# Whole-array attention and gate products in a fused windowed-attention and routed-MoE kernel

## The chip, the cores and the metric

The kernel runs on one core of a Trainium2 chip. The metric is device microseconds of one launch, the median of three runs. Before the change that is 237.91 us (237.64 to 238.76). The engines are named as the profile names them: PE is TensorE (PEld its weight loads), DVE is VectorE, ACT is ScalarE, POOL is GpSimd and SP is SyncE. A product means one matrix multiply instruction of PE; it multiplies a stationary operand, brought in by a weight load of its own, with a moving operand, and the number of partitions that both cover is called its rows here.

## The reference

```python
# q, k, v: (8, 8, 576, 64); window 32; scale 1/8
scores = where(abs(i - j) <= 32, scale * q @ k.T, -1e9)
attn   = softmax(scores)            # with + 1e-9 in the divisor
x      = (attn @ v)  ->  (4608, 512)     # 8 batches of 576 tokens, 8 heads of 64
# routed MoE: D=512, 8 experts, F=1024, 2 modalities
logits = x @ w_gate + modality_bias[modality_id]
e      = argmax(logits);  g = softmax(logits)[e]
out    = g * (relu(x @ w1[e]) @ w2[e])
```

The bias by modality is large beside the logits. The kernel works from the guess that all tokens of a modality go to the expert that the bias favours, flags any token or value that breaks its assumptions, and keeps a slow path behind that flag (attend and forward, from line 920), which the profiled execution does not enter.

## The kernel before

**Attention.** A batch has 8 heads, handled in two groups g of four (one load of q and one of k each), and in pairs of heads. Operation l loads a group as bf16 rows from POOL's queue, and t (L582) transposes it on DVE in 32x32 blocks. SA and SB (scores, L614) are the score products: 32 rows each (a head's 64 values lie as 32 rows times two columns), four heads side by side in the four row strips, with keys on the output partitions. Keys are cut in five blocks of 128 per head. For odd heads the blocks start 64 positions earlier, since 576 is four and a half blocks: the even head's last block holds keys in its first 64 partitions only, and the odd head's first block in its last 64 only. The other 64 partitions of such a block are the dead half. sa and sb (exps) take the exponential on ACT from PSUM into the probability tile pt; sb has a second activation (L625) for each head's block at the end of the tile (slot NM - 1), which is the half-dead one for even and odd heads alike. The scores of the six first pairs are masked by adding a band of large negative numbers in PSUM first (MA, MB, L591 and L595); from pair 6 on, M (L639) multiplies pt with a 0/1 band on DVE.

**V** (L659) multiplies the probabilities with the values: 18 products for a pair of heads, the probabilities stationary and 65 columns moving (64 values and a one, which gives the softmax sum). Two of the 18 cover the half-dead blocks and take 64 rows only, by the slice k_ of line 658. They are not neighbours: in the order of issue a product of 128 rows lies between them and follows each. v (L669, L670) takes the reciprocal and scales on DVE into x.

**Sorting.** The tokens of each 128-token block are sorted by modality: H (L679) multiplies x with a one-hot matrix (o, L573 on POOL or L576 on DVE), and a (L697) copies the result on ACT to a place in the table xl that depends on the counts. J and j (L710, L718) do the same with four rows of token codes, into the code table cl, which has 4 partitions and 4736 columns.

**MoE.** G (L748, L751) is the gate: for each 128 tokens four products of 128 rows and 8 columns, and one of 4 rows and 1 column that decodes the token's code from cl with the weights wi. There are 37 such groups, four to a G but for the last. r and E are the small softmax steps behind it. U (L821) and u (L834 on DVE, L836 on ACT) are the first expert layer, D (L844) and y (L857, L859) the second with the gate factor, O (L865) scatters the rows to the output by indirect DMA from POOL.

**Order.** The program is one list written out by hand or by a planner, the string ORDER (line 38). The loop at L914 reads it from left to right; each name issues its instructions to its engine's queue, and each engine works its queue in that order, waiting on semaphores. A number behind a colon names the PSUM banks used, a letter behind a slash the engine (a ACT, v DVE, p POOL). So the list sets what is queued behind what on every engine. K names are set-up steps: Kw clears zero_b, Kc7 clears a part of cl (384 columns at L415, on POOL), Kp clears the unused columns of a pt tile (L315, L316), Kh and Ki bring the modality table in and Kd converts it. X (L910) issues two products of 512 columns on the zeros of zero_b into a bank that nobody reads; the list has four X, ahead of everything else on PE.

Of the kernel before, what the change touches and what calls it, by code (L numbers as in the profile page):

```python
# [43 lines left out]
j0.1 j0.2 j0.3 Kp2/a j0.4 MA1.0:4567 SA1.0:4567 tv1.0 sb1.1 sa1.0 Ky1 Kb/p W1.0 o1/p l3.0.0 l2.0.1 l2.1.1 tv2.0 tv1.1
t2.0.0 t2.0.1 TV1.0:012 H0.1:3 SA1.1:4567 vc1.0/a sa1.1 H0.0:2 V5:01 TV1.1:456 v5 vc1.1/v H0.2:7 a0.0 a0.1 H0.4:2 V4:01
M6 v4 H0.3:3 a0.2 a0.3 a0.4 TV2.0:567 vc2.0/a V6:34 v6 U1.2:2 J1:01 u1.2/v SA2.0:3456 j1.0 j1.1 j1.2 sa2.0 j1.3 j1.4
U1.1:7 U1.0:2 tv2.1 M7 l3.1.0 W2.1 u1.0/v SB2.0:3456 u1.1/a V7:01 U0.1:2 v7 sb2.0 l3.0.1 Kc5 G0:7 l3.1.1 W2.0 l4.0.0
H1.0:0 u0.1/v H1.1:1 r0.5 r0.0 M8 U0.2:3 H1.2:5 u0.2/v H1.3:2 U1.3:4 H1.4:3 a1.0 a1.1 a1.2 a1.3 a1.4 TV2.1:567 U0.0:0
U2.2:3 G1:1 vc2.1/a t2.1.0 t2.1.1 r0.1 u1.3/v r1.0 r1.1 r1.5 M9 r1.2 t3.0.0 u2.2/a u0.0/a SB2.1:4567 V8:23 l4.1.0 o2/p
sb2.1 U2.1:0 U2.3:1 u2.1/a u2.3/a SA2.1:4567 sa2.1 v8 r0.2 t3.0.1 U2.0:0 V9:12 D1.1.0:3 E0 SA3.0:4567 D1.1.1:3 r0.3 v9  # L50
M11 r0.4 r1.7 D1.0.0:2 u2.0/a sa3.0 y1.1/a SB3.0:4567 sb3.0 E1 V11:01 t3.1.1 U3.2:3 D1.0.1:2 J2:45 U0.3:6 U3.0:7 M10 v11
r0.7 t3.1.0 u3.2/a u0.3/v y1.0/v j2.0 j2.1 j2.2 j2.3 u3.0/a j2.4 D2.1.0:0 V10:67 SA3.1:1234 sa3.1 t4.0.0 v10 r1.3
D0.1.0:5 D2.1.1:0 D0.1.1:5 y0.1/a SB3.1:1234 H2.1:6 t4.0.1 M12 r1.4 y2.1/v D2.0.0:7 H2.0:5 sb3.1 D2.0.1:7 D0.0.0:0 lv3.0
o4/p Kc6 lv3.1 H2.4:1 H2.3:4 H2.2:2 a2.0 a2.1 a2.2 a2.3 M13 V13:56 D0.0.1:0 V12:23 y2.0/v M14 l4.0.1 r0.6 Kf0 l4.1.1
l5.0.0 v13 v12 M15 y0.0/a a2.4 SB4.0:4567 U3.3:0 V14:12 U3.1:3 v14 sb4.0 t4.1.0 SA4.0:4567 u3.1/a u3.3/a o5/p O1.1
l5.1.0 O1.0 sa4.0 U4.0:1 V15:23 D3.0.0:0 t4.1.1 SB4.1:4567 v15 D3.0.1:0 U4.3:2 G2:3 sb4.1 SA4.1:4567 sa4.1 y3.0/a lv4.0
lv4.1 u4.0/v r1.6 M16 M17 r2.5 O0.1 o3/p Kc8 O2.1 r2.0 U5.1:1 D3.1.0:3 l5.1.1 l5.0.1 H3.1:7 H3.0:4 H3.2:5 u5.1/v a3.0
a3.1 H3.4:0 O0.0 l6.0.0 U5.2:1 H3.3:4 D3.1.1:3 V16:67 t5.0.1 u4.3/v M18 a3.2 a3.3 u5.2/a a3.4 U4.1:2 r2.1 r2.2 M19 v16
t5.0.0 J3:45 U4.2:1 U7.0:0 j3.0 j3.1 u4.1/a j3.2 j3.3 y3.1/a j3.4 E2 u7.0/a U5.0:2 V17:67 D4.0.0:3 u4.2/v v17 Ko1 V18:01
r2.3 r2.4 u5.0/v v18 r2.7 SA5.0:4567 sa5.0 D4.0.1:3 l6.0.1 l6.1.0 O2.0 l6.1.1 lv5.0 lv5.1 r2.6 y4.0/a U5.3:2 u5.3/a  # L60
SB5.0:4567 U7.2:0 U7.1:1 t5.1.1 t5.1.0 V19:23 u7.1/v u7.2/v sb5.0 M20 v19 SB5.1:4567 sb5.1 D4.1.0:1 D5.1.0:0 D4.1.1:1
SA5.1:2345 sa5.1 y4.1/v G3:6 D5.1.1:0 H4.0:1 H4.1:7 a4.0 a4.1 J4:23 H4.2:4 D5.0.0:5 a4.2 H4.3:1 a4.3 j4.0 t6.0.1 r3.5
t6.0.0 y5.1/a j4.1 U7.3:7 Kf2 O3.0 l7.1.1 l7.0.1 l7.1.0 Z1 U6.0:4 U6.3:1 M23 r3.0 M22 r3.1 u7.3/v u6.0/v r3.2 M21
D5.0.1:5 V20:67 u6.3/a E3 j4.2 j4.3 j4.4 v20 r3.3 t6.1.0 U6.2:0 V21:23 H4.4:1 v21 r3.4 y5.0/a u6.2/a a4.4 SB6.0:4567
sb6.0 U6.1:0 U8.1:1 V23:23 SA6.0:4567 u8.1/a v23 t6.1.1 u6.1/a sa6.0 U8.2:1 V22:23 D7.0.0:0 v22 M25 t7.0.1 SA6.1:4567
u8.2/a sa6.1 D7.0.1:0 H5.1:1 D7.1.0:3 SB6.1:4567 G4:2 y7.0/v sb6.1 r4.5 r4.0 t7.1.1 M24 r4.1 M26 M27 r4.2 r4.7 O3.1 O4.0
U8.3:0 D7.1.1:3 O4.1 lv6.0 lv6.1 r3.6 O7.0 l7.0.0 H5.3:4 H5.0:2 a5.0 y7.1/a O5.0 o7/p O7.1 lv7.1 O5.1 D6.0.0:5 a5.1
u8.3/a U9.1:7 H5.2:2 a5.2 a5.3 U8.0:3 D6.0.1:5 U9.0:0 J5:12 u9.1/v o6/v D6.1.0:4 V24:67 j5.0 j5.1 y6.0/a D6.1.1:4 j5.2
y6.1/a t7.1.0 u8.0/v v24 U9.2:3 V27:56 U9.3:7 j5.3 j5.4 u9.0/a E4 H5.4:0 v27 r4.3 t7.0.0 V26:12 v26 O6.1 lv7.0 r4.6 O6.0
u9.2/a a5.4 SB7.1:3456 D8.0.0:0 u9.3/a sb7.1 D9.0.0:7 V25:12 v25 r4.4 SA7.1:3456 D9.0.1:7 U10.1:1 D8.0.1:0 sa7.1  # L70
SB7.0:2345 D8.1.0:6 sb7.0 u10.1/v U10.0:1 D8.1.1:6 u10.0/a SA7.0:2345 y8.0/a r3.7 y8.1/v M30 sa7.0 U11.2:1 H6.0:0
U11.0:6 u11.2/a V30:23 u11.0/v H6.3:1 G5:4 v30 H6.1:5 a6.0 D9.1.0:0 H6.2:2 U11.1:3 H6.4:6 a6.1 y9.0/a a6.2 a6.3 u11.1/v
M29 M28 a6.4 U10.2:5 D9.1.1:0 J6:12 U13.2:7 u10.2/a r5.0 r5.1 M31 D10.1.0:3 V28:56 v28 j6.0 j6.1 j6.2 u13.2/a j6.3
U10.3:7 j6.4 y9.1/a G6:2 V29:01 V31:56 u10.3/a r6.0 r6.1 r6.2 v29 r6.7 r5.2 v31 E5 r5.3 U13.1:7 r5.4 r5.5 U12.0:0
D10.1.1:3 y10.1/a D11.0.0:5 H7.0:1 a7.0 H7.1:3 a7.1 H7.2:4 D10.0.0:6 U11.3:1 Z0 u11.3/v u13.1/v H7.3:3 D10.0.1:6
D11.1.0:1 u12.0/a D11.0.1:5 U12.2:0 u12.2/a a7.2 a7.3 r5.6 O10.1 O8.0 O9.1 O8.1 y10.0/v O10.0 O9.0 D11.1.1:1 y11.1/v
r6.5 H7.4:0 a7.4 U12.3:6 U13.3:1 J7:23 Kf3:0 Kf4 y11.0/v r5.7 u12.3/a U14.3:4 U13.0:6 U17.0:7 E6 j7.0 j7.1 j7.2 u13.0/a
j7.3 j7.4 U14.0:0 U12.1:2 G7:3 r6.3 u13.3/v Kf1 r7.0 u12.1/v r7.1 r7.5 r7.2 E7 u14.3/a r7.3 D13.1.0:1 D13.0.0:6 U14.1:5
D13.0.1:6 D13.1.1:1 U14.2:2 G8:3 r7.4 r8.5 r6.4 r8.0 u14.0/a r8.1 r8.2 u14.1/v y13.1/v D12.1.0:0 D12.0.0:4 U16.1:3
U16.3:1 D14.0.0:5 y13.0/a U17.3:6 D12.1.1:0 u17.3/a E8 u14.2/a D12.0.1:4 U16.0:2 u16.0/a u16.1/a u17.0/v y12.0/v O11.1  # L80
W1.2 D14.1.0:6 U18.0:4 U17.1:2 u17.1/a D14.1.1:6 D14.0.1:5 U16.2:2 U18.1:3 U17.2:7 y12.1/v D17.0.0:0 r8.3 u18.0/v W2.2
r6.6 O13.1 r8.6 N O11.0 O13.0 u16.3/v O12.0 G9:1 y14.0/v r7.7 U15.0:4 D17.1.0:5 u17.2/v D17.0.1:0 r8.4 y17.0/a u18.1/a
r9.0 r8.7 y14.1/v r9.5 r9.1 r9.2 r9.7 u16.2/a D17.1.1:5 y17.1/v D16.0.0:1 U15.3:3 Z6 r7.6 O14.0 r9.6 O14.1 U15.1:0 E9
# [7 lines left out]
def kernel(  # L91
# [527 lines left out]
    def exps(b, g, part):  # L619
# [4 lines left out]
        if part:  # L624
            nc.scalar.activation(pt[:, :, NM - 1, 0:WL], st[:, :, 2 * WIN:2 * WIN + WL], ACT.Exp, scale=scale)  # L625
# [18 lines left out]
    def V(_, it):  # L644
# [3 lines left out]
        for h in range(2):  # L648
            g0 = R // 2 * hp + (NM - 1) * h
            for m in range(NM):  # L650
# [6 lines left out]
                for i_, (j, c1) in enumerate(mine):  # L657
                    k_ = slice(0, 64) if h == 0 and j == NM - 1 else slice(64, P) if h == 1 and j == 0 else slice(0, P)
                    nc.tensor.matmul(  # L659
                        o_ap, pt[k_, c1:c1 + P], vt[k_, g0 + j, 0:D + 1],  # L660
# [80 lines left out]
    def G_(_, k_):  # L741
        lg = bank([P, 4, E + 1])
        hs = halves(k_)
        for n_, t_, s_ in hs:
# [6 lines left out]
            ins = nc.tensor.matmul(lg[:, n_, E:E + 1], cl[:, c0:c0 + P], wi[0:4, i_, :],  # L751
# [333 lines left out]
```

## Time and profile before

| What | Value |
|---|---|
| Median of three runs | 237.91 us |
| The profiled execution's own time | 239.17 us |
| Its span in the profile | 237.5 us |
| Mean granted PE clock | 0.985 |
| Last products of L844 begin | 229.42 us |
| Products of V with 64 rows | 64 of 576 |
| Gate products with 4 rows | 37 |

The span is shorter than the execution by what lies around the program. A busy time is the union of the instructions of an engine. PE's instructions overlap: one lasts some 200 ns in the record although the next may begin 30 ns later, so PE's durations cannot be added up; what counts is the distance between starts, which the chain of waits and short stretches of the timeline show. The chain of waits is followed back from the end of the program and gives each stretch of time to the instruction that the next step waited for.

### The profile page before, as it was taken

The numbers are of one execution on the slowest core, as the hardware profiler recorded it, in microseconds if no ns is written. First come the engines' busy times: TensorE is split into PE (matmuls) and PEld (weight loads), VectorE is DVE, ScalarE is ACT, GpSimd is POOL, SyncE is SP. The second block draws the span as 40 slices with busy tenths as digits, with TensorE's granted clock in tenths as the row PEclk, the third lists the DMA queues.
The fourth block names the chain that finished last, engine by engine and source line by source line (L and its number), as shares of the span: only waits on it lengthen the run. The fifth ranks groups of instructions, "written<-read, shape, count | busy, mean of one in ns | idle before, by whom it ended". The sixth has DMA issues, their size and how long they took to land.

```text
span 237.5 us, 6484 instructions
## 1 busy us (share of the span) xinstructions
PE 220.1 (93%) x2676; PEld 155.8 (66%) x2676; DVE 151.9 (64%) x296; ACT 138.5 (58%) x220; POOL 122.8 (52%) x223
## 2 busy tenths in 40 slices
PE   7497789999999999999999999999999899999980
...
DVE  1979689868988697687886785435653453244330
...
GB/s 77 201 180 191 205 217 204 211 211 211 177 96 0 74 157 70 195 218 200 263 81 0 53 88 157 124 0 3 0 3 177 134 123 204 76 134 88 125 104 98
DMA packets 34054, 30.44 MB, mean 128 GB/s; under 512 B 24888, under 2 KB 24928, under 8 KB 33632
## 3 DMA queue, kind: packets, MB, share of 16 engines
...
HBM read 40.96 MB, written 9.70 MB: 213 GB/s over the span
## 4 chain that ended last, share of the span: by engine, by line
PE 81%; issue 4%; DVE 4%; POOL 3%; ACT 3%; DMA 2%; POOLq 0%; DVEq 0%
PE banks L821 27%; PE banks L844 24%; PE banks L659 12%; PE banks L614 6%; PE banks L679 4%; PE banks L252 3%; PE banks L748 3%; POOL out_dram L865 2%; DMA qkin<-in_q_dram 2%; PE banks L751 2%; ACT pt L622 1%; PE banks L710 1%; DVE xt L670 1%; PE banks L591 1%; DVE vt L268 1%
## 5 line engine op out<-in xcount | busy, mean ns | idle before, releaser
L821 PE MATMUL banks<-xl,w_sb 128*128 128x256 bf16 x576 | 72.2, 273 | 0.8 <-issue 0.6
L844 PE MATMUL banks<-w_sb,hT 128*128 128x512 bf16 x288 | 70.4, 379 | 0.1
L865 POOL DMA_INDIRECT out_dram<-ys,ix x37 | 39.8, 1075 | 46.3 <-issue 37.6
L821 PEld LDWEIGHTS <-w_sb 128*128 128x128 bf16 x576 | 53.9, 98 | 12.2 <-issue 2.3
L622 ACT ACTIVATE pt<-banks 128x1536 bf16<-128x1536 f32 x32 | 46.3, 1449 | 26.0 <-PE banks L614 24.1
L844 PEld LDWEIGHTS <-hT 128*128 128x128 bf16 x296 | 27.0, 98 | 25.0 <-issue 0.8
L582 DVE STREAM_TRANSPOSE qk<-qkin 128x576 int32<-128x576 int32 x32 | 38.8, 1245 | 4.7 <-DMA qkin<-in_k_dram 4.3
L659 PE MATMUL banks<-vt,pt 128*128 128x65 bf16 x576 | 36.1, 195 | 1.6 <-DVE xt L670 1.2
L836 ACT ACTIVATE hT<-banks 128x512 bf16<-128x512 f32 x44 | 25.3, 594 | 18.0 <-PE banks L821 12.9
L659 PEld LDWEIGHTS <-pt 128*128 128x128 bf16 x576 | 28.8, 97 | 9.9 <-issue 1.7
L697 ACT CAST xl<-banks 128x704 f32 (+1 forms) x40 | 28.5, 712 | 11.4 <-PE banks L679 9.7
L573 POOL TENSOR_SCALAR oh<-io_l,lpf 128x128 bf16<-128x128 bf16 x35 | 24.3, 706 | 15.5 <-PE banks L679 15.3
L834 DVE TENSOR_SCALAR hT<-banks 128x512 bf16<-128x512 f32 x30 | 20.3, 683 | 16.0 <-PE banks L821 15.5
L639 DVE TENSOR_TENSOR pt<-pt,mask 128x1920 bf16<-128x1920 bf16 x26 | 29.7, 1150 | 0.0
L670 DVE TENSOR_TENSOR xt<-banks,recs 128x640 bf16<-128x640 f32 x32 | 26.4, 824 | 1.2
L857 ACT ACTIVATE ys<-banks,gw 128x512 f32<-128x512 f32 x19 | 13.0, 683 | 24.3 <-PE banks L844 20.0
L859 DVE TENSOR_SCALAR ys<-banks,gw 128x512 f32<-128x512 f32 x18 | 13.3, 744 | 17.6 <-ACT hT L836 7.9
L614 PE MATMUL banks<-qk 32*128 32x192 bf16 (+1 forms) x640 | 18.4, 239 | 2.0 <-DVE qk L582 1.9
L669 DVE RECIPROCAL recs<-banks 128x10 f32<-128x10 f32 x32 | 7.0, 217 | 17.2 <-PE banks L659 15.3
L614 PEld LDWEIGHTS <-qk 32*128 32x128 bf16 x640 | 12.3, 92 | 8.4 <-issue 5.1
L783 POOL CAST ix<-ixf 128x4 int32<-128x4 f32 (+1 forms) x10 | 2.2, 217 | 28.1 <-DVE ixf L780 25.7
L718 ACT CAST cl<-banks 4x176 f32 (+1 forms) x40 | 11.3, 283 | 3.5 <-PE banks L710 1.6
...
## 6 DMA issues: line engine op xcount, KB each, us to landing
...
out_dram<-ys,ix POOLq DMA_INDIRECT x37
mid<-in_moe_modality_id_dram SPq DMA_DIRECT2D x3, 8.0 KB
```

The lines of the kernel that those rows point to most:

```text
L573: gp.tensor_scalar(out=t_[:, m, :], in0=io_l[:], scalar1=lpf[:, NM * b + m:NM * b + m + 1], scalar2=None, op0=ALU.is_equal)
L582: nc.vector.transpose(qk_t[b % 2][:, g, at:at + S].rearrange("p (t r) -> p r t", r=R), Ct["l", b, u, g][:].bitcast(I32).rearrange("p (r j) ...
L614: nc.tensor.matmul(st[:, h, WIN * i_:WIN * i_ + w_], qk[32 * h:32 * h + 32, c_, QK + k0:QK + k0 + P], qk[32 * h:32 * h + 32, c_, q0:q0 + w ...
L622: nc.scalar.activation(pt[:, :, 2 * part:2 * part + 2, 0:WIN], st[:, :, 0:2 * WIN].rearrange("p h (j c) -> p h j c", c=WIN), ACT.Exp, scal ...
L639: by[eng or "v"].tensor_tensor(out=p_ap, in0=p_ap, in1=mask[:], op=ALU.mult)
L659: nc.tensor.matmul(o_ap, pt[k_, c1:c1 + P], vt[k_, g0 + j, 0:D + 1], start=(m == 0 and i_ == 0), stop=(i_ == len(mine) - 1), skip_group_ch ...
L670: nc.vector.tensor_tensor(out=x_t[b % NX][:, :, P * hp:P * hp + P].rearrange("p m (h d) -> p h m d", h=2), in0=o_v[:, :, :, 0:D], in1=rec. ...
L697: ins = nc.scalar.copy(windows(xl, n_kd, P, NM * b + m), src)
L821: ins = nc.tensor.matmul(ph[:, u_, :], w1[:, kd, 2 * P * (mi // 2) + mi % 2:2 * P * (mi // 2 + 1):2], xl[:, kd, c0:c0 + n_], start=(kd == ...
L836: nc.scalar.activation(o_ap, i_ap, ACT.Relu)
L844: nc.tensor.matmul(Ct["D", t_, s_], Ct["h", t_][:, kf, P * s_:P * s_ + P], w2[:, kf, :], start=(kf == 0), stop=(kf == n_kf - 1))
L865: ins = nc.gpsimd.indirect_dma_start(out=out, out_offset=bass.IndirectOffsetOnAxis(ap=ix[:, k_, n_:n_ + 1], axis=0), in_=Ct["y", t_, s_][: ...
```

## The change

Three edits give all products of V and G 128 rows.

1. V drops the slice, so its 64-row products run over whole blocks. The dead half must hold zeros for this: Kp now clears slot NM - 1 from column 0 instead of 128, and sb's second activation becomes two, one for the even heads' first 64 partitions and one for the odd heads' last 64, which leave the dead halves alone.
2. cl and the weights wi are used with 128 partitions instead of 4. cl is allocated that tall and cleared whole by one DVE memset; it was 4 partitions by 384 columns on POOL.
3. The list ORDER is replaced by another, which holds the same operations and ten more X (14 in all). Nearly all steps change places; counts by engine change in u (45 on ACT and 29 on DVE, from 44 and 30), o (6 on POOL and 2 on DVE, from 7 and 1), Kp (2 on ACT and one on DVE, from 3 and none) and Kv (2 on POOL and 2 on DVE, from 3 and 1).

```diff
-Kh Kw X0:7 X1:6 X2:5 X3:4 l0.1.0 l0.0.0 Kv3/p Kn0 lw0.0 Kj MA0.0:4567 Km Ki t0.0.1 t0.0.0 Ke Kv1/v Kx tv0.0 Kd
-MB0.0:0123 l0.0.1 l0.1.1 Kv2/p l1.0.0 Kv0/p Kc7 Kp1/a Kq0/a Kq1/a Kp0/a t0.1.0 SA0.0:4567 SB0.0:0123 sa0.0 sb0.0 lw0.1
...
+Km l0.1.0 Kw Kc7 Kj l0.0.0 lw0.0 Kn0 Ke Kh Kx Kq0/a t0.0.1 t0.0.0 X4:7 X3:2 X0:4 X2:3 MB0.0:4567 Ky0 Kp1/v Kv2/v X9:2
+X11:3 X10:2 X5:3 SB0.0:4567 X6:3 Ki MA0.0:0123 SA0.0:0123 Kd tv0.0 Kv0/v l0.0.1 t0.1.0 Kp0/a sb0.0 sa0.0 Kv1/p l0.1.1
+t0.1.1 lw0.1 Kc1 Kq1/a l1.1.0 l1.0.0 Kc4 Kc0 Kv3/p Kc3 Kc2 TV0.0:567 vc0.0/a Kt0:4 Kr0 MB0.1:0123 SB0.1:0123 l1.1.1
+Kt1:4 sb0.1 tv0.1 X7:5 TV0.1:567 Kr1 t1.0.1 MA0.1:0123 SA0.1:0123 Kt2:4 t1.0.0 Kr2 vc0.1/a sa0.1 V0:67 V1:45 v0 v1
...
-    cl = const.tile([4, TOP], BF16, name="cl")
+    cl = const.tile([P, TOP], BF16, name="cl")
...
-            pad(eng, p_t[i][:].rearrange("p (h j c) -> p h j c", h=4, c=SW)[:, :, NM - 1, WL:WIN])
+            pad(eng, p_t[i][:].rearrange("p (h j c) -> p h j c", h=4, c=SW)[:, :, NM - 1, 0:WIN])
...
-            gs.memset(cl[:, N // 2 - T3:N // 2 + 2 * T3], 0.0)
+            nc.vector.memset(cl[:], 0.0)
...
-            nc.scalar.activation(pt[:, :, NM - 1, 0:WL], st[:, :, 2 * WIN:2 * WIN + WL], ACT.Exp, scale=scale)
+            for h, p0 in ((0, 0), (1, 64)):
+                nc.scalar.activation(pt[p0:p0 + 64, h::2, NM - 1, 0:WL], st[p0:p0 + 64, h::2, 2 * WIN:2 * WIN + WL],
+                                     ACT.Exp, scale=scale)
...
-                    k_ = slice(0, 64) if h == 0 and j == NM - 1 else slice(64, P) if h == 1 and j == 0 else slice(0, P)
                     nc.tensor.matmul(
-                        o_ap, pt[k_, c1:c1 + P], vt[k_, g0 + j, 0:D + 1],
+                        o_ap, pt[:, c1:c1 + P], vt[:, g0 + j, 0:D + 1],
...
-            ins = nc.tensor.matmul(lg[:, n_, E:E + 1], cl[:, c0:c0 + P], wi[0:4, i_, :],
+            ins = nc.tensor.matmul(lg[:, n_, E:E + 1], cl[:, c0:c0 + P], wi[:, i_, :],
```

More of the change, by code (lines that the diff above doesn't have):

```diff
@@ L44 @@
[L44 to L83, printed above, removed]
@@ new lines @@
+t3.1.0 sb3.0 D1.1.0:6 D1.0.1:5 U3.2:0 y1.0/v Ko1 V10:12 D1.1.1:6 V11:34 y1.1/a U3.0:5 U3.3:6 u3.3/a u3.2/v v10 v11
+SA3.1:0123 u3.0/v J2:45 sa3.1 j2.0 j2.1 j2.2 D2.0.0:7 U3.1:6 SB3.1:0123 D2.0.1:7 M12 r1.7 r1.3 t4.0.1 r1.4 y2.0/v M13
+j2.3 u3.1/a j2.4 D0.1.0:6 H2.1:5 H2.2:4 H2.0:7 D0.1.1:6 sb3.1 V13:12 D2.1.0:0 y0.1/v t4.0.0 v13 H2.3:3 a2.0 a2.1 a2.2
+D2.1.1:0 y2.1/a a2.3 M15 SB4.0:4567 V12:12 D0.0.0:0 H2.4:3 sb4.0 D0.0.1:0 v12 M14 lv3.1 V15:12 y0.0/v v15 l4.1.1 r0.6
+t4.1.1 SA4.0:4567 l4.0.1 O1.1 a2.4 U4.2:3 u4.2/a U4.0:0 u4.0/a sa4.0 r1.6 l5.1.0 lv4.0 O1.0 o3/p l5.0.0 t4.1.0 U4.3:1
@@ new lines @@
+U5.3:0 V14:23 SB4.1:4567 u5.3/v sb4.1 v14 U4.1:0 G2:2 U5.2:3 u5.2/a SA4.1:4567 sa4.1 u4.1/a l5.1.1 lv4.1 u4.3/v r2.5
+r2.0 t5.0.1 D3.1.0:1 U5.0:2 H3.1:3 H3.0:5 u5.0/a D3.1.1:1 H3.4:0 H3.2:2 H3.3:4 J3:67 a3.0 a3.1 j3.0 a3.2 D3.0.0:5 M17
+y3.1/v M16 t5.0.0 U5.1:1 j3.1 a3.3 V17:23 D3.0.1:5 a3.4 j3.2 y3.0/a j3.3 U7.2:4 u7.2/a j3.4 U7.3:0 u7.3/a u5.1/a r2.1
+M18 v17 V16:23 SA5.0:4567 U7.0:0 U7.1:1 l5.0.1 M19 Kc6 O0.1 O2.0 Z1 l6.1.0 o4/p O0.0 v16 t5.1.1 r2.2 V19:23 sa5.0 v19
+SB5.0:4567 u7.1/a u7.0/a sb5.0 D4.0.0:1 D4.1.0:0 V18:23 t5.1.0 E2 v18 SB5.1:4567 D4.0.1:1 G3:2 D5.1.0:3 sb5.1 SA5.1:4567
@@ new lines @@
+r2.3 o5/v r2.4 r3.5 r3.0 r3.1 l6.0.0 O3.1 r2.6 O2.1 sa5.1 D4.1.1:0 H4.0:2 D5.1.1:3 a4.0 J4:45 r3.2 r3.7 t6.0.1 y4.0/v E3
+j4.0 lv5.0 lv5.1 j4.1 t6.0.0 D7.0.0:1 H4.4:2 D7.0.1:1 H4.2:6 D5.0.0:7 r3.3 r3.4 y5.1/v j4.2 j4.3 j4.4 y4.1/a H4.1:0 a4.1
+a4.2 H4.3:3 a4.3 D5.0.1:7 a4.4 U6.1:0 M23 M21 M20 r2.7 M22 y7.0/a y5.0/a V21:45 v21 u6.1/v U6.0:6 V20:23 v20 U8.1:1
+D7.1.0:0 SB6.0:2345 sb6.0 u6.0/v u8.1/v D7.1.1:0 V23:67 U9.0:1 G4:5 U8.0:2 V22:34 l6.0.1 v23 o6/v r4.0 t6.1.0 v22 O4.0
+o7/p r3.6 l6.1.1 O3.0 O7.0 l7.0.1 O4.1 l7.0.0 l7.1.1 lv6.1 O5.1 U8.2:6 U9.3:7 u9.3/v t6.1.1 u9.0/a u8.0/a y7.1/a
@@ new lines @@
+SA6.0:0123 U8.3:4 u8.2/a sa6.0 u8.3/v U9.2:6 SA6.1:0123 H5.0:4 r4.1 t7.1.0 r4.5 u9.2/a U6.2:7 U9.1:6 u9.1/v sa6.1
+SB6.1:0123 U6.3:5 t7.0.0 u6.3/v u6.2/a a5.0 H5.2:7 D6.1.0:4 D8.0.0:6 sb6.1 H5.1:0 J5:12 D8.0.1:6 D6.1.1:4 a5.1 a5.2
+D6.0.0:0 H5.3:5 D9.0.0:3 D6.0.1:0 H5.4:7 D9.0.1:3 lv6.0 Kf0 M26 r4.2 r4.7 t7.1.1 E4 j5.0 j5.1 j5.2 j5.3 y6.1/a j5.4 a5.3
+r4.3 M25 r4.4 M27 V26:12 y8.0/v M24 a5.4 y9.0/a D8.1.0:4 v26 y6.0/a V27:56 SB7.1:0123 v27 U10.2:7 D8.1.1:4 V24:56
+u10.2/v O7.1 l7.1.0 r4.6 O5.0 lv7.0 O9.0 lv7.1 Kf2 O8.0 O6.0 O6.1 U11.3:7 v24 u11.3/v t7.0.1 sb7.1 y8.1/a SA7.1:0123
@@ new lines @@
+H7.1:6 H7.2:7 O9.1 u13.3/v u12.3/a D13.0.0:0 U12.2:4 O8.1 r5.6 O10.0 N O11.1 O10.1 u13.2/v E6 a7.1 j7.0 j7.1 j7.2 a7.2
+r6.3 u12.2/v D13.0.1:0 H7.3:1 D12.1.0:4 D11.0.1:5 y11.0/v O11.0 j7.3 j7.4 a7.3 H7.4:1 a7.4 D13.1.0:2 D12.0.0:3 D13.1.1:2
+D12.1.1:4 D12.0.1:3 Kf3:1 r6.4 r6.7 G7:5 Kf4 U14.1:6 U16.0:7 U17.2:1 u14.1/v u17.2/a U15.2:6 u15.2/a y12.1/v y13.0/v
+U15.3:0 G9:6 G8:1 r7.0 r7.5 r8.5 y13.1/a U17.3:2 r7.6 r6.6 r8.6 U15.1:5 r7.1 r8.0 y12.0/v r7.2 r7.7 U14.2:4 U14.0:1
+u14.0/a U17.0:3 u17.0/a U14.3:1 E7 u15.1/a u17.3/a u14.3/a u14.2/a D14.1.0:3 D14.0.0:5 U17.1:1 U15.0:4 D14.0.1:5 r7.3
```

25 lines of the change are left out of this document (19 added, 6 removed).

## The prediction, made before the changed kernel was run

> **What bounds the kernel now.** I read the page first (busy shares, the 40 slices), then busy time by stage, then the groups by shape, and last the timeline and the chain of waits inside the products that change.
>
> ```profile
> span 237.5 us, 6484 instructions
> PE 220.1 (93%) x2676; PEld 155.8 (66%) x2676; DVE 151.9 (64%) x296; ACT 138.5 (58%) x220; POOL 122.8 (52%) x223
> PE   7497789999999999999999999999999899999980
> DVE  1979689868988697687886785435653453244330
> ...
> 30.00:40.00 10.00, 9.05 (x158) 7.94 (x157) 8.88 (x12) 8.35 (x9) 7.40 (x18) 1.00 1.03 212
> 40.00:60.00 20.00, 19.98 (x313) 16.52 (x315) 16.32 (x29) 15.78 (x24) 14.03 (x36) 1.00 1.13 210
> 80.00:100.00 20.00, 20.00 (x283) 15.33 (x271) 16.81 (x25) 15.23 (x25) 18.68 (x21) 1.00 0.91 134
> 40.00:220.00 180.00, 179.11 (x2152) 128.30 (x2151) 118.77 (x227) 107.35 (x175) 82.14 (x120) 1.00 0.69 118
> ```
>
> The last four rows are stages: PE, PEld, DVE, ACT and POOL busy, then granted clock, DMA share and GB/s. Two kernels lie one behind the other. Until about 40 us PE has holes. From 40 to 220 us it has a product under way for 179.11 of 180 us, so only 0.9 us there is open waiting. DVE, the next engine, has 16.81 of 20 us at its fullest (84%), ACT 15.78 (79%).
>
> A PE that is always busy need not be working, since a product's record lasts far longer than its turn. So I ask how far apart the starts are.
>
> ```profile
> L659 PE MATMUL banks<-vt,pt 128*128 128x65 bf16 x512 | 31.9, 195 | 1.6 <-DVE xt L670 1.2 <-DVE cA L500 0.3
> L659 PEld LDWEIGHTS <-pt 128*128 128x128 bf16 x512 | 22.9, 97 | 6.9 <-issue 1.7
> L659 PE MATMUL banks<-vt,pt 64*128 64x65 bf16 x64 | 12.8, 201 | 0.0
> L751 PE MATMUL banks<-wi,cl 4*128 4x1 bf16 x37 | 6.4, 172 | 0.0
> ```
>
> ```profile
> 170.85 0.25 PE L748 MATMUL banks<-wg_sb,xl 128*128 128x8 bf16 x4
> 171.03 0.17 PE L751 MATMUL banks<-wi,cl 4*128 4x1 bf16 x1
> ...
> 171.43 0.39 PE L659 MATMUL banks<-vt,pt 128*128 128x65 bf16 x7
> ```
>
> ```profile
> 171.10 0.10 PE banks L751
> 171.21 0.19 PE banks L748 x4
> 171.39 0.10 PE banks L751
> 171.50 2.04 PE banks L659 x36
> ```
>
> These are groups by shape (count | busy us, mean ns | idle before), the timeline (start, length) and the chain, which gives each product only the time until the next step. Seven V products in a row, all of 128 rows, last 0.39 us from the first start to the last end. Less one product's 195 ns that is six distances in 0.195 us, 33 ns each. Yet in the chain two whole V (36 products, four of them with 64 rows) take 2.04 us, where 36 distances of 33 ns make 1.19. The other 0.85 us stands beside four products, 0.21 us each: a stall on the way into the 64-row form and another on the way out. The gate shows the same. Four products and the 4-row one take 0.19 + 0.10 = 0.29 us in the chain; inside the four the distance is (0.25 - 0.17) / 3 = 27 ns, and five of those make 0.13. That is 0.16 us for each L751.
>
> **The change part by part.** *Products.* V: 64 x 0.21 = 13.4 us. Gate: 37 x 0.16 = 5.9 us. Together 19.3 us of PE time go. How much of it lies where PE sets the pace?
>
> ```profile
> 0.00:20.00 20.00, 2.27 (x36) 1.77 (x36) 0.91 0.91 158
> 20.00:40.00 20.00, 5.70 (x90) 4.34 (x90) 1.00 1.07 205
> ...
> 0.00:40.00 40.00, 0.00 (x0) 0.00 (x0) 0.96 0.99 181
> ```
>
> The first two rows are L659 alone, the third L751 alone (busy PE and PEld, clock, DMA). Before 40 us lie 126 of the 576 V products, 7 of 32 V, and no gate. The 25 later V give 25 x 0.42 = 10.5 and the gates 5.9: 16.4 us, counted in full, since PE waits for nothing else there. The 7 early V are worth 2.9 us at most, and nothing where another engine holds them; I take half, 1.5.
>
> *Exponentials.* sb's second activation, of 512 elements, becomes two of 256.
>
> ```profile
> L622 ACT ACTIVATE pt<-banks 128x1536 bf16<-128x1536 f32 x32 | 46.3, 1449 | 26.0 <-PE banks L614 24.1 <-DVE xt L670 1.8
> L625 ACT ACTIVATE pt<-banks 128x512 bf16<-128x512 f32 x16 | 9.5, 593 | 0.0
> ```
>
> From 1449 and 593 ns an element costs 0.84 ns and a start 165 ns, so each half takes 380 ns and the pair 165 ns more than before: 16 x 0.165 = 2.6 us of ACT, which idles 26 us before L622 alone. For V it is 0.17 us of latency per sb. The list puts other products between sb and its V, so I count 0.3 us (bounds 0 and 2.6; all of it if that cover is gone).
>
> *Clearing.* cl's clear moves to DVE, ahead of its first transpose, and grows to 4736 columns. One pt pad moves from ACT to DVE, behind the second transpose.
>
> ```profile
> 1.31 0.27 DVE L303 MEMSET zero_b<- 128x256 uint32 x1
> 5.86 1.26 DVE L582 STREAM_TRANSPOSE qk<-qkin 128x576 int32<-128x576 int32 x1 [4.27 <-DMA qkin<-in_k_dram]
> ...
> 8.69 0.18 DVE L424 MEMSET e<- 128x1 f32 x8
> 8.93 0.11 DVE L437 TENSOR_REDUCE pm<-mb_bc 128x2 f32<-128x16 f32 x1
> 9.70 0.17 DVE L442 TENSOR_SCALAR sp_i<-ext_e 128x2 int32<-128x2 f32 x1
> ```
>
> zero_b's 512 bf16 went as 256 words in 0.27 us, so cl's 2368 words take 2.5. From about 1.4 us on that ends near 3.9. The steps put behind it, Ke (0.18), Kh (some 0.27) and Kx (0.94, from 8.93 to 9.87), end near 5.3, before the first load lets the transpose start at 5.86: free. Element by element the clear would take 5.0 and push the transpose to 7.8, so the bounds are 0 and 1.9 us. I take 0, as zero_b's row is the same instruction. The pad has 1280 and 768 elements: 1.1 us as words, 2.2 as elements, in a stage where DVE is 89% busy (8.88 of 10). I count 0.5. The Trainium skill, "VectorE: DVE Perf Modes", section "Zero memsets can be issued as uint32 (trn2)", says that a zero clear of whole, aligned 4-byte words can go as words. By it this term is 0.5 us; without it, 2 to 3.
>
> *Zeros and clock.* The ten new X are 20 products of 512 columns, all ahead of the first U of the list, so in the early stage.
>
> ```profile
> 10.00:12.00 2.00, 0.87 (x13) 0.84 (x14) 2.00 (x3) 2.00 (x2) 1.74 (x8) 0.93 1.11 209
> 12.00:14.00 2.00, 2.00 (x17) 1.49 (x15) 1.87 (x6) 1.44 (x3) 1.48 (x9) 0.50 1.10 207
> 14.00:16.00 2.00, 2.00 (x38) 1.36 (x36) 1.68 (x5) 0.44 (x2) 1.85 (x5) 0.72 1.04 178
> ```
>
> ```profile
> 11.32 1.85 PE banks L252 x20
> 13.46 1.39 PE banks L591 x4
> 20.89 1.29 PE banks L252 x20
> 22.18 0.65 PE banks L591 x4
> 175.29 1.73 PE banks L844 x8
> ```
>
> At 0.22 us each (1.73 / 8, also 512 columns) they take 4.3 us, nothing where they fill holes. After a hole (PE busy 0.87 us from 10 to 12) the granted clock is half from 11.7 to 15.1 us, by the 0.93, 0.50 and 0.72 of the three stages. The chain shows the price: the same two groups take 1.85 + 1.39 us then and 1.29 + 0.65 later, 1.3 us. If the X keep the clock up this goes; if they stand in the way, as much is lost. I take a gain of 0.6.
>
> *New order.* Every step moves, so waits are dealt anew. Kd, which waits for the modality table that Ki now fetches later, stands on DVE ahead of tv0.0; queued behind it are the value transpose and t0.1.0, and TV and the first V wait for those. So the first V comes later, but V0 to V3 stand closer together. I count nothing for it, with 2 us either way. The last steps of the list (D16.1, y16.1, O16.1) stay. From 40 us on, less PE time makes the other engines denser; I let PE's 0.9 us of open waiting grow by 1.0.
>
> Sum: 16.4 + 1.5 + 0.6 - 0.3 - 0.5 - 1.0 = 16.7 us. The profiled execution took 239.17 us (its span and 1.7 around it), so 222.5 by its own time. The median is 237.91 us, 1.3 lower for the same work: 237.9 - 16.7 = **221.2 us**.
>
> **The rivals.** *DVE takes over (0.22).* From 40 to 140 us DVE is at 82 to 84%, some 82 us of work. PE's 9% less would make those 100 us 91 and ask 90% of DVE. If it can't go beyond the 84% that it has now, they become 98, and 6 us come back: 227. For: the list takes no work off DVE. Against: PE has no open wait for it there today.
>
> *The start gains too (0.13).* All 2.9 us of the early V, all 1.3 of the clock and 2 from closer V: 217. For: the holes are there. Against: loads keep the DMA full until 60 us (shares of 0.91 to 1.13).
>
> *Loads come bare (0.02).* If a load into rows that a product is using had to wait for it, each changed product would pay its 97 ns load: 64 x 0.11 + 37 x 0.06 = 9.3 us of gain in all, some 7 after the costs, 231. Against: the seven products at 33 ns distance, whose loads are recorded at 97 ns. The Trainium skill, "TensorE: Matmul & The Clock Gate", section "Part 3: Packing small matmuls — row/col tiling", says that a load overlaps products under way only where the row groups differ. The trace contradicts it, by those 33 ns.
>
> *The new order stalls PE: slower (0.04).* PE takes its queue in order, so one product that waits for an exponential or for v holds all behind it. V and the two score steps per group make 64 such places. At 0.26 us more for each, the 16.7 us are gone and it decides; at 0.35 the time is 244. Against: L659's row shows 1.6 us of idle in all.
>
> *The gaps have another cause than the row count (0.02).* Then nothing goes, and X and pads find holes: 238.
>
> **How the numbers follow.** A measurement of this kernel can tell about 0.5% from no change. My forecast has 0.57, its own range 218 to 224.5 (the bounds above, without the far end of the exponentials). The range of 8 in 10 reaches into the two large rivals: 215.5 to 228. Faster holds the forecast, the takeover, the start and the bare loads, 0.94; the same 0.02; slower 0.04.
>
> **What would show it.** Two V side by side near 1.2 us in the chain; a gate group near 0.13 us without steps of 0.10 for L751; PE still with a product under way nearly always from 40 us on; L625 32 times at about 380 ns; one clear of cl of about 2.5 us that ends before the first transpose; no half clock at 12 us. It is wrong if V keeps steps of 0.2 us, or if PE's idle time before L659 and L614 grows to several us behind DVE or ACT.

## The result and the profile after

| What | Before | Changed |
|---|---|---|
| Median of the runs side by side | 237.77 us | 224.05 us |
| Lowest to highest | 237.42 to 238.76 | 222.65 to 224.63 |
| Profiled execution | 239.17 us | 223.96 us |
| Its span | 237.5 us | 222.3 us |
| Mean granted PE clock | 0.985 | 0.986 |

The ratio is 0.9408, with a 95% interval of 0.9356 to 0.946. The change gains 13.7 us by medians and 15.2 us by the two profiled executions; 221.2 us (a gain of 16.7) had been forecast. Two of the executions of the experiments below, one of gate_only (307.84 us) and one of after_again (347.43), ran at a mean clock of 0.65 and 0.56 and are left out of the medians.

The profile page of the changed kernel, busy shares and slices (line numbers behind L625 are one higher than before):

```profile
span 222.3 us, 6507 instructions
PE 204.5 (92%) x2669; PEld 145.6 (66%) x2696; DVE 154.7 (70%) x302; ACT 141.0 (63%) x234; POOL 118.7 (53%) x215
PE   6759888999999999999999999999999999999960
DVE  6677999896977998697997879686775236312420
PEclk9978999999999999999999999999999999999997
```

Its busy time by stage (PE, PEld, DVE, ACT, POOL, then clock, DMA share, GB/s):

```profile
40.00:60.00 20.00, 19.27 (x333) 16.02 (x332) 17.32 (x29) 17.36 (x25) 8.52 (x15) 1.00 1.10 212
80.00:100.00 20.00, 19.89 (x296) 15.96 (x295) 16.68 (x25) 16.24 (x27) 15.00 (x23) 1.00 0.88 147
100.00:120.00 20.00, 19.79 (x278) 12.87 (x280) 17.56 (x33) 14.53 (x26) 8.02 (x10) 1.00 0.57 64
40.00:205.00 165.00, 163.21 (x2130) 118.74 (x2149) 117.97 (x228) 109.18 (x185) 77.31 (x116) 1.00 0.80 133
```

PE still has a product under way nearly always from 40 us on: 1.8 us open in 165, where before it was 0.9 in 180. DVE now reaches 17.56 of 20 us (88%), above the 84% that it had before.

The products that changed, in the groups by shape, and then in the chain of waits:

```profile
L660 PE MATMUL banks<-vt,pt 128*128 128x65 bf16 x576 | 22.6, 193 | 0.0
L626 ACT ACTIVATE pt<-banks 64x256 bf16<-64x256 f32 x32 | 11.9, 371 | 0.4
```

```profile
120.20 0.55 PE banks L660 x18
...
121.62 0.08 PE banks L749 x4
121.70 0.02 PE banks L752
121.73 0.10 PE banks L749 x4
121.83 0.02 PE banks L752
121.85 0.10 PE banks L749 x4
...
161.26 1.10 PE banks L660 x36
```

All 576 V products now have one shape. A V alone takes 0.55 us and two side by side 1.10, where two took 2.04. A gate group takes 0.12 us, of which the decoding product has 0.02 instead of 0.10. A single V of before, in the same view, stood at:

```profile
99.85 0.97 PE banks L659 x18
```

So a V got cheaper by 0.97 - 0.55 = 0.42 us, which is the price that the prediction put on its four stalls.

**Where the time went.** The first U is a place at which the two lists have nearly the same work behind them: seven V, the scores of two batches, no gate. The new list has one J more there (0.34 us a J, in the chain of before). The timelines of before and of the changed kernel:

```profile
39.16 1.03 PE L821 MATMUL banks<-xl,w_sb 128*128 128x256 bf16 x8
```

```profile
40.76 1.05 PE L822 MATMUL banks<-xl,w_sb 128*128 128x256 bf16 x8 [0.28 <-DMA w_sb<-in_moe_w_dram]
```

From there to the end of the span before takes 237.5 - 39.16 = 198.3 us and the changed kernel 222.3 - 40.76 = 181.5: 16.8 us gained, against 16.4 counted for the late products. order_only, told of below, has the new list with the old products and takes 238.1 - 40.54 = 197.6 us from there, 16.1 more than the changed kernel; the late gain is as sure as these two figures agree. Up to there it *loses* 1.6 us, although seven V got cheaper in that stretch too. The late part came about as worked out; the start did not. What follows tells how far the reasons are known.

### The profile page after: what moved, and what is told of

Same layout as the page of the kernel before. It is cut to its first block, busy times and chain, and to the rows that moved or that the text cites. A ratio compares the mean times of both kernels' runs of the same rounds, so it can differ in the third digit from the quotient of the medians.

```text
span 222.3 us, 6507 instructions
## 1 busy us (share of the span) xinstructions
PE 204.5 (92%) x2669; PEld 145.6 (66%) x2696; DVE 154.7 (70%) x302; ACT 141.0 (63%) x234; POOL 118.7 (53%) x215
## 4 chain that ended last, share of the span: by engine, by line
PE 76%; DMA 9%; POOL 6%; issue 2%; DVE 2%; SPq 1%; POOLq 0%; DVEq 0%
PE banks L845 28%; PE banks L822 28%; DMA w_sb<-in_moe_w_dram 6%; PE banks L660 6%; PE banks L614 5%; POOL oh L573 3%; PE banks L680 3%; DMA mid<-in_moe_modality_id_dram 2%; PE banks L749 2%; PE banks L711 1%; DVE cl L415 1%; POOL out_dram L866 1%; SPq L285 1%; PE banks L252 1%; POOL qkin L217 1%
## 5 line engine op out<-in xcount | busy, mean ns | idle before, releaser
L866 POOL DMA_INDIRECT out_dram<-ys,ix x37 | 38.9, 1051 | 70.4 <-issue 27.9
L822 PE MATMUL banks<-xl,w_sb 128*128 128x256 bf16 x576 | 70.7, 273 | 0.7 <-DMA w_sb<-in_moe_w_dram 0.7
L845 PE MATMUL banks<-w_sb,hT 128*128 128x512 bf16 x267 | 67.7, 379 | 1.1
L835 DVE TENSOR_SCALAR hT<-banks 128x512 bf16<-128x512 f32 x29 | 19.6, 682 | 9.0 <-PE banks L822 7.9
L660 PEld LDWEIGHTS <-pt 128*128 128x128 bf16 x576 | 21.1, 97 | 2.8 <-DVE pt L641 0.2
L660 PE MATMUL banks<-vt,pt 128*128 128x65 bf16 x576 | 22.6, 193 | 0.0
L573 POOL TENSOR_SCALAR oh<-io_l,lpf 128x128 bf16<-128x128 bf16 x30 | 19.9, 682 | 2.7 <-PE banks L680 1.9
L860 DVE TENSOR_SCALAR ys<-banks,gw 128x512 f32<-128x512 f32 x18 | 13.2, 743 | 10.6 <-PE banks L845 10.5
L217 POOL DMA_DIRECT2D qkin<-in_k_dram x16 | 10.3, 642 | 12.1 <-DMA w_sb<-in_moe_w_dram 7.8
L680 PEld LDWEIGHTS <-xt 128*128 128x128 bf16 x160 | 11.2, 114 | 4.6 <-issue 0.7
L222 POOL DMA_DIRECT2D vt<-in_v_dram x10 | 13.7, 1373 | 0.0
```

What stands on the lines that cost most here:

```text
L573: gp.tensor_scalar(out=t_[:, m, :], in0=io_l[:], scalar1=lpf[:, NM * b + m:NM * b + m + 1], scalar2=None, op0=ALU.is_equal)
L660: nc.tensor.matmul(o_ap, pt[:, c1:c1 + P], vt[:, g0 + j, 0:D + 1], start=(m == 0 and i_ == 0), stop=(i_ == len(mine) - 1), skip_group_chec ...
L822: ins = nc.tensor.matmul(ph[:, u_, :], w1[:, kd, 2 * P * (mi // 2) + mi % 2:2 * P * (mi // 2 + 1):2], xl[:, kd, c0:c0 + n_], start=(kd == ...
L845: nc.tensor.matmul(Ct["D", t_, s_], Ct["h", t_][:, kf, P * s_:P * s_ + P], w2[:, kf, :], start=(kf == 0), stop=(kf == n_kf - 1))
L866: ins = nc.gpsimd.indirect_dma_start(out=out, out_offset=bass.IndirectOffsetOnAxis(ap=ix[:, k_, n_:n_ + 1], axis=0), in_=Ct["y", t_, s_][: ...
```

## The experiments

The kernels of each of the three groups below shared one chip and were compared with the kernel before on it. In the expectations A is the theory of the prediction, that PE stalls at each change of the row count; the other letters are rivals and later theories, told where they are first used. The chip of the second group ran the kernel before at 240.53 us, so its times are compared by their ratios.

### First group: the products and the list, each alone (before: 237.66 us)

**v_only**: the old list, with only V at 128 rows.

```diff
-pad(... [:, :, NM - 1, WL:WIN])
+pad(... [:, :, NM - 1, 0:WIN])
-nc.scalar.activation(pt[:, :, NM - 1, 0:WL], ...)
+the two activations by halves, as in the change
-o_ap, pt[k_, c1:c1 + P], vt[k_, g0 + j, 0:D + 1],
+o_ap, pt[:, c1:c1 + P], vt[:, g0 + j, 0:D + 1],
```

> The old list with V alone at 128 rows (and the dead halves kept zero). Theory A, that each change of the row count costs a stall: 25 late V save 0.42 us each, 10.5 us, the 7 early ones 0 to 2.9, the split exponentials take 0.3: 224.7 to 227.6 us. Rival B, that most of the gain comes from the new list: over 232 us.

Measured: 224.98 us, ratio 0.9446 (0.9378 to 0.9513). V alone gives 12.7 us, as theory A had it. From its first U (37.33 us) to the end of its span (224.6) it takes 187.3 us, 11.1 less than before, where 10.5 were counted.

**gate_only**: the old list, with only the gate's last product at 128 rows, and cl cleared whole on DVE right behind Kw.

```diff
-Kh Kw X0:7 X1:6 ... Kv0/p Kc7 Kp1/a
+Kh Kw Kc7 X0:7 X1:6 ... Kv0/p Kp1/a
-cl = const.tile([4, TOP], BF16, name="cl")
+cl = const.tile([P, TOP], BF16, name="cl")
-gs.memset(cl[:, N // 2 - T3:N // 2 + 2 * T3], 0.0)
+nc.vector.memset(cl[:], 0.0)
-wi[0:4, i_, :]
+wi[:, i_, :]
```

> The old list with the gate's last product alone at 128 rows; cl is cleared on DVE right behind Kw. Theory A: 37 x 0.16 = 5.9 us less, all of it where PE sets the pace, and nothing or little lost at the start by the 2 us clear: 231.5 to 233.5 us. Rival B: over 236 us.

Measured: 232.99 us, ratio 0.9754 (0.963 to 0.9879). The gate gives 4.7 us by the medians and 5.8 by the ratio, from few executions; the interval (2.9 to 8.8) holds the 5.9 counted. The first U is at 39.80 us, 0.6 later than before, and from there to the end of the span (231.4) it takes 191.6 us, 6.7 less.

**both_old_order**: both edits, the old list with its four X.

> All products at 128 rows in the old list with its four X. Theory A, with no part for the list: 10.5 + 5.9 us less and half of the early V, 219.5 to 222.5 us, which would be faster than the changed kernel's 224.05. Rival C, that the old list, made for other lengths, now makes PE wait: 224 to 230 us.

Measured: 220.05 us (218.87 to 220.65), ratio 0.9226 (0.915 to 0.9303). Together the two edits gain 17.6 us, where each alone gave 12.7 and 4.7. This is the best kernel of the study, 4 us below the changed one.

**order_only**: the new list with its fourteen X, and the old products.

> The new list with the old products (64 rows in V, 4 in the gate, the old clears). Theory A: the list by itself gains nothing and its start costs some: 237.5 to 241 us. Rival B: under 234 us.

Measured: 239.39 us, ratio 1.007 (1.0033 to 1.0106). With the old products the new list costs 1.7 us, and the interval (0.8 to 2.5 us) leaves out zero. With the new products it costs 220.05 against 224.05, about 4 us.

### Second group: is it the change of the row count? And what in the list costs? (before: 240.53 us)

**adjacent**: the kernel before, with all its 64-row products kept, but the two of a V issued next to each other.

```diff
-mine = [(m, SW * m)] + [(m - 1, SW * (m - 1) + P)] * (m > 0)
+mine = [(m - 1, SW * (m - 1) + P)] * (m > 0) + [(m, SW * m)]
```

> The kernel before, with the 64-row products kept, but the two of a V next to each other (the last block of the even head comes second in its sum). Theory A, that the stall belongs to each change of the row count: two changes a V instead of four, so half of the 0.42 us goes, 25 x 0.21 = 5.2 us and up to 1.5 of the early V: 231 to 232.6 us. Rival D, that each short product is itself 0.2 us dearer: 237 to 238.5 us.

Measured: 233.3 us, ratio 0.9746 (0.9682 to 0.9811), a gain of 6.1 us by the ratio (4.5 to 7.7), as theory A had it. In its chain of waits:

```profile
81.66 0.74 PE banks L659 x18
...
166.13 1.58 PE banks L659 x36
```

A V falls from 0.97 to 0.74 us, although it does the same products with the same rows. Only the number of changes between 128 and 64 rows went down, from four to two. So the stall belongs to the change of the row count and not to a short product: 0.97 - 0.74 = 0.23 us for two changes fewer and 0.74 - 0.55 = 0.19 for the two that are left, some 0.1 us each. Two V side by side say the same: 2.04, 1.58 and 1.10 us, so 0.23 and 0.24 us for a V.

**no_x**: the changed kernel without the ten added X.

```diff
-X9:2 X11:3 X10:2 X5:3 ... X6:3 ... X7:5 ... X13:6 ... X1:3 ... X8:3 ... X12:2
```

> The changed kernel with the four old X only; the ten new ones are out. Theory E, that the new X stand in PE's way between 30 and 40 us, where five or six of their products of 0.22 us are ahead of work that is ready: 222.5 to 223.2 us. Rival F, that they keep the clock up and fill holes: 224.5 to 226 us.

Measured: 229.32 us, ratio 0.9563 (0.9518 to 0.9608), more than either theory allowed.

**kh_first**: the changed kernel, with Kh and Ki (the modality table) ahead of Kc7 (the clear of cl), and Kd behind tv0.0 and t0.1.0.

```diff
-Km l0.1.0 Kw Kc7 Kj ... Ke Kh Kx ... X6:3 Ki MA0.0:0123 SA0.0:0123 Kd tv0.0 Kv0/v l0.0.1 t0.1.0 Kp0/a
+Km l0.1.0 Kw Kh Ki Kc7 Kj ... Ke Kx ... X6:3 MA0.0:0123 SA0.0:0123 tv0.0 Kv0/v l0.0.1 t0.1.0 Kd Kp0/a
```

> The changed kernel with Kh and Ki ahead of Kc7, and Kd behind tv0.0 and t0.1.0, so that the value transpose no longer stands behind the late modality table. Theory G, that the hole of 2.5 us before TV at 13.9 us is a good part of what the new list costs: 222 to 223.3 us, and no hole there. Rival H, that what comes later (loads, weights) sets the pace anyway: 223.5 to 224.5 us.

Measured: 227.92 us, ratio 0.9504 (0.9458 to 0.955), again more than either theory allowed.

**w_early**: the changed kernel, with the weight load W1.1 moved ahead of o0 and o1 on POOL.

```diff
-Kr3 Kc5 o0/p lw2.0 ... lw2.1 W1.1 l2.1.1
+Kr3 Kc5 W1.1 o0/p lw2.0 ... lw2.1 l2.1.1
```

> The changed kernel with the first weight load W1.1 ahead of POOL's one-hot steps o0 and o1, so that the DMA is not empty from 20 to 25 us. Theory I, that the weights are late: the waits of L822 for w_sb (0.7 us in all) go and the first U comes at or before 39 us: 222.3 to 223.4 us. Rival J, that other loads are put back by as much: 223.6 to 225 us.

Measured: 231.3 us, ratio 0.9654 (0.9604 to 0.9704), the slowest of the three; the expectation failed. The load was issued at 21.55 us instead of 29.81, but the first U came at 45.18 us. The timeline of w_early, and its windows:

```profile
45.18 1.06 PE L822 MATMUL banks<-xl,w_sb 128*128 128x256 bf16 x8
```

```profile
10.00:22.00 12.00, 9.54 (x107) 6.03 (x107) 7.20 (x19) 6.27 (x9) 8.20 (x33) 0.57 1.05 190
34.00:40.00 6.00, 5.04 (x70) 3.79 (x71) 5.36 (x7) 3.88 (x6) 5.55 (x11) 0.72 1.15 197
```

PE ran at half clock for some 10 of the 12 us (0.57) and once more before 40 us (0.72). The test mixes an earlier load with a slower clock, so it does not tell whether the weights hold the new list.

In this group the changed kernel itself was not run, and its three variants all came out slower by ratio than its own 0.9408. That called for a run of them side by side.

### Third group: side by side with the changed kernel (before: 238.56 us)

Theory K, below, is that the new list starts the expert layers some 3 us late and never gets it back. **after_again** is the changed kernel, **both_old_again** is both_old_order, **no_x_again** is no_x, and **no_x_kh** is no_x with the edit of kh_first.

> The changed kernel itself, beside the next three on one chip, since the last call's kernels had a slower kernel before (240.53 us) than the first (237.66). If the stalls of 1.3 to 1.6 us near 120, 150 and 170 us that two kernels of the last call show belong to the chip, they are here too and the ratio is 0.95 to 0.96; if they belong to the edits, the ratio is 0.935 to 0.946 as on record.

> All products at 128 rows in the old list, a second time. Theory K, that the new list starts the expert layers 3 us later and never gets it back: 3 to 4 us less than the run beside it of the changed kernel. Rival: within 1 us of it.

> The changed kernel without the ten new X, a second time. Theory E, that they stand in the way: 0.7 to 1.5 us less than the changed kernel beside it. Rival F, that they pay by the clock: 1 us or more above it.

> The changed kernel without the ten X and with Kh and Ki first and Kd behind t0.1.0. If the late first U (40.8 us, 37.6 in the old list) is made of the X (0.8 us) and of the hole at the modality table (1.5 us), the first U starts at 38.3 to 38.9 us and the time is 1.5 to 2.5 us below the changed kernel beside it; if weights or loads hold what follows, the first U is early and the time is within 1 us of it.

| Kernel | us | Ratio (interval) | First U (its first weight load), us | From there to the span's end |
|---|---|---|---|---|
| after_again | 223.73 | 0.9383 (0.9337 to 0.9428) | 40.86 | 181.3 |
| both_old_again | 219.4 | 0.9224 (0.9172 to 0.9277) | 36.11 | 181.9 |
| no_x_again | 225.3 | 0.9448 (0.9399 to 0.9498) | 41.62 | 181.4 |
| no_x_kh | 223.38 | 0.937 (0.9327 to 0.9412) | 40.38 | 181.4 |

The last column is the span less the first U (222.2, 218.0, 223.0 and 221.8). It is the same for all four within 0.6 us. The difference between the lists, 4.3 us by the medians and 4.2 by these spans, is all there when the first U starts (40.86 against 36.11), as theory K had it. The windows that end and begin there show the same. First after_again, the last row being the X alone, then both_old_again with its row of X, then no_x_again:

```profile
0.00:40.86 40.86, 32.25 (x480) 21.58 (x486) 32.75 (x67) 28.22 (x45) 33.42 (x90) 0.96 0.88 154
40.86:222.20 181.34, 172.49 (x2194) 123.89 (x2213) 122.07 (x237) 112.81 (x190) 85.76 (x125) 0.99 0.76 133
...
0.00:40.86 40.86, 8.04 (x23) 2.74 (x28) 0.96 0.88 154
```

```profile
0.00:36.11 36.11, 25.57 (x459) 18.71 (x460) 29.74 (x59) 29.17 (x44) 32.10 (x90) 1.00 0.99 183
36.11:218.00 181.89, 172.73 (x2200) 124.02 (x2219) 122.44 (x239) 112.65 (x193) 92.83 (x134) 0.99 0.74 131
...
0.00:36.11 36.11, 3.60 (x8) 1.04 (x8) 1.00 0.99 183
```

```profile
0.00:41.62 41.62, 30.38 (x464) 21.10 (x465) 33.02 (x67) 28.19 (x45) 33.31 (x90) 0.88 0.86 150
```

Ahead of the first U the new list has 32.25 - 25.57 = 6.7 us more PE busy time, 4.4 of it in X. Without the ten X that time does not come back: the mean clock falls from 0.96 to 0.88. At half clock as the only other value that is 2 x 0.12 x 41.62 = 10 us of half clock instead of 2 x 0.04 x 40.86 = 3.3. The other executions bear it out: the mean clock of the whole span is 0.958 to 0.974 in the six of no_x_again and 0.979 to 0.992 in the five of after_again. So the X keep the clock up, as rival F had it. What they take and what they save nearly cancel: no_x_again is 1.6 us slower by the medians, with intervals that overlap.

no_x and no_x_again are one kernel, at ratios of 0.9563 and 0.9448 whose intervals do not meet. In no_x PE has no product under way for 1.2 us near 121, 0.7 near 150 and 1.4 near 171 us; kh_first and w_early have holes of the same lengths at the same steps, and no_x_again misses at most 0.11 us in any 5 us from 80 to 215 us. So these 3.3 us of the second group belong to that chip, with the new list, and not to the edits, and its ratios cannot be set against 0.9408. The ratio of after_again is the one expected if the holes belonged to the edits, but no_x_again has that edit and no holes. What makes them is not known.

**The clear of cl is not free in the new list.** no_x_kh is 1.9 us faster than no_x_again by the medians (their intervals just meet), and its first U comes 1.2 us earlier. Its expectation failed all the same: the first U was to come by 38.9 us and came at 40.38, and the time is only 0.35 us below after_again. The only difference in the list is that Kh and Ki stand ahead of the clear, and Kd behind two transposes. Why that matters is seen in the timelines of DVE and of SP's queue, first of order_only (the new list, the small clear on POOL), then of the changed kernel, then of kh_first:

```profile
1.46 0.27 DVE L290 MEMSET mid<- 40x256 int32 x1
...
11.26 0.45 DVE L467 CAST midr<-mid 40x128 bf16<-40x128 int32 x1
...
4.57 0.62 SPq L286 DMA_DIRECT2D mid<-in_moe_modality_id_dram  x1
```

```profile
1.77 2.03 DVE L415 MEMSET cl<- 128x2368 uint32 x1 [0.44 <-issue]
...
3.90 0.27 DVE L290 MEMSET mid<- 40x256 int32 x1
...
12.43 0.22 DVE L467 CAST midr<-mid 40x128 bf16<-40x128 int32 x1 [2.03 <-DMA mid<-in_moe_modality_id_dram]
12.58 1.24 DVE L239 STREAM_TRANSPOSE xl<-qkin 128x576 int32<-128x576 int32 x1
...
7.01 0.62 SPq L286 DMA_DIRECT2D mid<-in_moe_modality_id_dram  x1
```

```profile
1.32 0.27 DVE L290 MEMSET mid<- 40x256 int32 x1
2.03 2.03 DVE L415 MEMSET cl<- 128x2368 uint32 x1 [0.44 <-issue]
...
14.15 0.20 DVE L467 CAST midr<-mid 40x128 bf16<-40x128 int32 x1
...
4.43 0.62 SPq L286 DMA_DIRECT2D mid<-in_moe_modality_id_dram  x1
```

Kh is a small clear of the table mid (L290), and the DMAs of Ki on SP write into that table, so they wait for it. With the big clear ahead of Kh, Kh comes 2.4 us later (3.90 against 1.46) and the last modality load is issued 2.4 us later (7.01 against 4.57). Then Kd waits 2.03 us for it on DVE (1.91 us in no_x_again), with tv0.0 and the transposes queued behind, and PE waits 2.50 us for the first of them. In order_only Kd does not wait, and in kh_first and no_x_kh it does not either. In kh_first the first U starts at 39.35 us, but a later U waits 1.46 us for its weights, so that the lead is lost again. The timeline of kh_first, products of U:

```profile
39.35 1.06 PE L822 MATMUL banks<-xl,w_sb 128*128 128x256 bf16 x8
...
48.11 1.92 PE L822 MATMUL banks<-xl,w_sb 128*128 128x256 bf16 x16 [1.46 <-DMA w_sb<-in_moe_w_dram]
```

## Why the prediction came out as it did

The forecast was 221.2 us in a range of 215.5 to 228, and 224.05 came. The main mechanism was right; two terms of the start were not. Step by step:

- **Late products, 16.4 us: right.** The stall sits at the change of the row count (adjacent), costs 0.42 us for a V (0.97 to 0.55), and v_only and both_old_order bring 12.7 and 17.6 us. Behind the first U the changed kernel gains 16.8 us, or 16.1 against order_only. Why a change costs this much no run shows.
- **Other engines denser, 1.0 us: the wait grew as forecast.** PE's open time from 40 us on is 1.8 us in 165, from 0.9 in 180. The 16.8 us are what is left after it, so the late part came out up to 1.4 us better than 16.4 - 1.0.
- **Exponentials, 0.3 us: size right.** L626 takes 371 ns each, 380 was forecast. What it costs in time was not tested alone; v_only, which holds it, brings 12.7 of the 13.4 us counted for all V. The pad on DVE also has the length forecast: the two clears of L324 take 1.01 us, 1.1 was worked out; what they cost in time was not tested either.
- **The DVE rival (84% is the most): refuted.** DVE runs at 88% from 100 to 120 us. The 82 to 84% that the prediction gives for before hold from 40 to 100 us (16.32 to 16.81 of 20); from 100 to 140 DVE was at 79 to 80% (15.90 and 15.86). The sum of some 82 us of work is right.
- **The other rivals.** Loads do not come bare: 0.55 us for 18 products are 31 ns each, against loads of 97. The rule of the Trainium skill, "TensorE: Matmul & The Clock Gate", section "Part 3: Packing small matmuls — row/col tiling", that a load overlaps products under way only where the row groups differ, does not hold here, as the trace of before had it. The gaps go with the changes of the row count (adjacent). The start did not gain, and the new list does not stall PE in its 64 places: behind the first U it is level with the old one.
- **The clear's cover, "The steps put behind it ... end near 5.3, before the first load lets the transpose start at 5.86: free": this step failed.** The clear went as words and took 2.03 us where 2.5 were forecast; it ends at 3.80 us and the steps behind it at 5.29, ahead of the first transpose at 5.88. That it can go as words is what the Trainium skill, "VectorE: DVE Perf Modes", section "Zero memsets can be issued as uint32 (trn2)", says. But what had to be counted was not when DVE is done with Kh, but what Kh releases: the modality loads on SP. The wait for the modality table was named in the part on the order, and its cause was not tied to the clear. In the pair no_x_again and no_x_kh the order of these steps is worth 1.9 us. That pair moves Kd as well and differs in half clock, so the clear's own share is not measured.
- **"New order ... I count nothing for it, with 2 us either way": mis-sized.** The list costs 1.7 us with the old products and 4.0 to 4.3 with the new ones, with the new ones all of it ahead of the first U. The place of the clear, worth 1.9 us with Kd's where it was measured (without the added X), can account for most of what lies between the two figures. That the first V comes later was foreseen, and it does (22.3 us in after_again, 14.1 in both_old_again), but V0 to V3 moving closer together did not make up for it.
- **Early V, 1.5 us: there on the old list, not seen on the new one.** On the old list the first U moves from 39.16 to 37.58 us in both_old_order, 1.6 us at the same 3.4 us of half clock, and to 36.14 in both_old_again, which has no half clock there. On the new list it is at 40.54 with the old products (order_only, at full clock) and at 40.76 with the new ones, which ran 3.4 us of it at half clock, so these two do not show the early V by themselves.
- **Clock, 0.6 us: no gain.** The half clock moved from 11.7-15.1 us to 14.4-17.8; it did not go:

```profile
12.00:14.00 2.00, 0.12 (x3) 0.13 (x4) 1.57 (x5) 1.89 (x4) 1.55 (x8) 1.00 1.11 210
14.00:16.00 2.00, 2.00 (x22) 1.67 (x21) 2.00 (x3) 0.26 (x1) 1.86 (x5) 0.61 1.11 194
16.00:18.00 2.00, 2.00 (x24) 1.21 (x26) 1.31 (x3) 0.87 (x1) 1.86 (x8) 0.54 1.06 182
```

 These are stages of the changed kernel. The hole before it (PE busy 0.12 of 2 us) is the wait for the modality table. order_only and kh_first, which have no such wait, show a clock of 1.00 in all five stages of 2 us from 10 to 20 us. But that the wait brings the half clock is not shown: both_old_order and both_old_again are one kernel, without that wait, and the first has half clock there and the second has none:

```profile
10.00:15.00 5.00, 3.64 (x41) 2.62 (x30) 4.82 (x14) 4.27 (x5) 4.08 (x16) 0.72 1.10 204
```

```profile
10.00:15.00 5.00, 3.97 (x75) 3.30 (x76) 4.77 (x12) 4.53 (x6) 4.04 (x16) 1.00 1.10 206
```

 So the prediction took the half clock of one execution of before for a fixed part of the kernel, and it changes from execution to execution. The first U comes 1.4 us earlier without it (36.14 against 37.58), near the 1.3 us that the prediction worked out as the most to be had.
- **The range.** The forecast's own 218 to 224.5 is narrower than the bounds of its terms: on the slow side the early V (1.5), the clear (1.9) and the order (2) alone would reach 226.6. That 224.05 still lies in it is in part luck, since the start came out 2.9 us worse than forecast and the late part up to 1.4 us better.

**The sum of the misses.** 16.7 forecast less 13.7 measured leaves 3.0 us. The start was forecast to gain 1.3 (1.5 + 0.6 - 0.3 - 0.5) and lost 1.6: 2.9 us. The late part came 1.4 us better. The other 1.5 us are no work of the change: the profiled execution of before was 1.4 us above its median and that of the changed kernel 0.1 below it. Where in that execution the 1.4 us lie is not known; measured against order_only the late part is 0.7 us better instead of 1.4.

**What stays open.** In order_only the first U comes 1.4 us later than before, at full clock, but no single step is shown to be the cause. Two things stand there together: ten X (4.4 us of PE) and weights issued 5 us later (29.52 us in order_only, 24.82 in both_old_again). In the changed kernel the wait for the modality table and the half clock come on top. Removing X brought half clock (no_x_again), an earlier table met late weights (kh_first), and earlier weights met half clock (w_early). That they hide one another is argued from these runs and not shown by one. A version with the old list's start and the new list's rest was not run; by the last column of the table it could gain 0.6 us at most over both_old_order. No run has the new products in the new list with the clear at another place alone or on another engine, which would price the clear.
